# A gated attention and feed-forward decode step: half of w_down on 128 partitions, V's end and wo in fewer pieces

## The chip, the core and the metric

The kernel runs on one core of a Trainium2 chip. The metric is the device time in microseconds (us) of one execution: the median of the runs, beside which one execution is profiled. PE is the matrix engine, DVE the vector engine, ACT the scalar engine, POOL the general one, and SP the engine that issues nearly all transfers. The core's transfers run on 16 DMA engines.

## The reference

One token attends to a cache of 65,536 positions in 32 heads; beside it runs a gated feed-forward layer, and a scalar gate mixes the two.

```
x [1,1,512]; k_cache, v_cache [1,32,65536,128]; wq [512,4096]; wo [4096,512]
w_gate, w_up [512,1792]; w_down [1792,512]; all bf16

g = sigmoid((x * gate_w).sum())
q = (x @ wq) as 32 heads of 128
p = softmax(q . k_cache / sqrt(128));  o = p @ v_cache
a = o (as 4096 values) @ wo
b = (silu(x @ w_gate) * (x @ w_up)) @ w_down
out = g * a + (1 - g) * b
```

K and V are 512 MiB each and are read once.

## The kernel before, in words

**Tiles.** Each head's cache is cut into G = 4 parts of 16,384 rows, so there are N = 128 tiles of K and 128 of V. A tile is 4 MB: 128 partitions with 128 rows (32 KB) each. The tiles live in a ring of five slots (`take`, `give`); a load takes the slot that has been free longest, so SP waits there until PE or DVE has done with the slot's last content. Each transfer on SP also uses one of eight semaphores in turn, and waits until the transfer eight before it has landed.

**K.** `products` (L254, L258) multiplies a K tile by the head's query on DVE and folds it to 32 columns (64 for the first head); `scores` (L267) sums these with identity matmuls into PSUM, and `fold` (L281) sums the rest. After a head's four tiles come its maximum, the exponentials (`P_sb`) and the total.

**V.** `values` (L322) runs 32 matmuls for each V tile, four rows of each partition at a time. They accumulate in `O_ps`, [4, 512] for a head. `head_copy` (L335) and `head_turn` (L351, L358) turn that into one column of `oT`, scaled. For the last tile, the last TURNED = 8 rows go straight into the turned sum (L343). `project` (L365) multiplies a head's column by its 128 rows of wo, two matmuls of 256 columns that accumulate in `a_ps`.

**Order.** A list `steps` pairs K tile n with V tile v; K runs ahead. In each step SP issues K, then perhaps a wo group, then V; PE does a finished head's `head_turn`, then `values`, `scores` and `project`. wo comes in groups of WG = 4 heads (512 KB, rows of 1 KB) into a pool of two buffers, for the first 16 heads; for the last 16 heads (`LATE`), 2 MB come behind the last V in four pieces (L169) into a ring slot, and `project` for these 16 heads stands at the end of PE's program. The last three V tiles come in pieces too (`V_CUTS`): two halves, two halves, and rows 0, 32, 64, 96, 112, 120, 128 of the last.

**Feed-forward.** It runs in the first 100 us. SP issues, in this order: the first columns of wq, K 0 to 2, the rest of wq, w_gate, K 3, w_up, six pieces of w_down, K 4, two pieces of w_down, V 0, K 5, V 1 and so on. `feed_forward_in` (L178) makes the 14 + 14 columns of gate and up, `feed_forward_mid` their product `hT` [128, 14]. w_down lies on 64 partitions with 28 rows each. It comes in eight transfers (L402) of eight partitions: `firsts[i]`, and then every fourth. `feed_forward_out` regroups `hT` to 64 partitions by two matmuls (L227) and a copy (L231), and runs 28 matmuls (L233) over w_down; then the slot `wd_t` is given back, for which SP waits before K 6.

Of the kernel before, what the change touches and what calls it, by code (L numbers as in the profile page):

```python
# [8 lines left out]
ACT = mybir.ActivationFunctionType  # L9
ALU = mybir.AluOpType  # L10
AXIS = mybir.AxisListType
P = 128
# [3 lines left out]
NB = 128  # L16
# [7 lines left out]
SPREAD = 40  # L24

WG = 4
LATE = 16
LATE_CUTS = (0, 5, 10, 14, LATE)
TURNED = 8
V_CUTS = {3: (0, 64, NB), 2: (0, 64, NB), 1: (0, 32, 64, 96, 112, NB - TURNED, NB)}  # L30


@with_exitstack
def kernel(
# [14 lines left out]
    nc = tc.nc  # L49
    bf16 = mybir.dt.bfloat16  # L50
    f32 = mybir.dt.float32

    _, H, Sk, Dh = A_k_cache.shape
    D = A_x.shape[2]
    F = B_w_gate.shape[1]
    KT = D // P
    FT = F // P
    G = Sk // (NB * P)
    NBH = Sk // P
    N = H * G  # L60
    QG = 4
    assert Dh == P and Sk % (NB * P) == 0 and NBH <= 512 and H % QG == 0 and G >= 2
    scale = float(Dh) ** -0.5

    consts = ctx.enter_context(tc.tile_pool(name="consts", bufs=1))
# [7 lines left out]
    psum_m = ctx.enter_context(tc.tile_pool(name="psum_m", bufs=2, space=bass.MemoryType.PSUM))  # L73
# [7 lines left out]
    def take(name):  # L81
        slot = free.pop(0)
        held[name] = slot
        return ring.tile(
            [P, NB * Dh], bf16, name=name.split(".")[0], tag=f"slot{slot}"
        )
# [4 lines left out]
    xT = consts.tile([P, KT], bf16, name="xT")  # L91
# [24 lines left out]
    def load_v(n):  # L116
        load(V_tiles, A_v_cache, n, "V_t", V_CUTS.get(N - n, (0, NB)))

# [9 lines left out]
    ident_b = consts.tile([P, P], bf16, name="ident_b")  # L128
# [29 lines left out]
    wo_tiles = {}  # L158

    def load_wo(g):  # L160
        wo_tiles[g] = wo_pool.tile([P, WG, D], bf16, name="wo_sb", tag="wo_sb")
        rows = A_wo[g * WG * P : (g + 1) * WG * P, :]
        nc.sync.dma_start(out=wo_tiles[g], in_=rows.rearrange("(h p) n -> p h n", p=P))

    def load_late(cuts):
        late = take("wo_late.0")[:, : LATE * D].rearrange("p (h n) -> p h n", n=D)
        rows = A_wo[(H - LATE) * P :, :].rearrange("(h p) n -> p h n", p=P)
        for a, b in zip(cuts[:-1], cuts[1:]):
            nc.sync.dma_start(out=late[:, a:b, :], in_=rows[:, a:b, :])  # L169
        return late  # L170

    def feed_forward_in():
        gu_ps = psum_m.tile([P, 2 * FT], f32, name="gu_ps", tag="misc")
        for w in range(2):
            cols = wgu_sb[:, w].rearrange("p t (m c) -> p t c m", c=FT)
            for ft in range(FT):
                for t in range(KT):
                    nc.tensor.matmul(  # L178
                        gu_ps[:, w * FT + ft : w * FT + ft + 1],
                        lhsT=cols[:, t, ft, :],  # L180
                        rhs=xT[:, t : t + 1],
                        start=(t == 0),
                        stop=(t == KT - 1),
                    )
        gu_sb = consts.tile([P, 2 * FT], f32, name="gu_sb")
        nc.scalar.activation(out=gu_sb, in_=gu_ps, func=ACT.Copy)
        eg = consts.tile([P, FT], f32, name="eg")
        nc.scalar.activation(out=eg, in_=gu_sb[:, :FT], func=ACT.Exp, scale=-1.0)
        return gu_sb, eg

    def gate_sum():
# [22 lines left out]
    def feed_forward_mid(gu_sb, eg):  # L214
        nc.vector.tensor_scalar_add(eg, eg, 1.0)
        nc.vector.reciprocal(eg, eg)
        hprod = consts.tile([P, FT], f32, name="hprod")
        nc.vector.tensor_tensor(out=hprod, in0=gu_sb[:, :FT], in1=eg, op=ALU.mult)
        hT = consts.tile([P, FT], bf16, name="hT")
        nc.vector.tensor_tensor(out=hT, in0=hprod, in1=gu_sb[:, FT:], op=ALU.mult)  # L220
        return hT

    def feed_forward_out(hT, rest):
        b_ps = psum_m.tile([1, D], f32, name="b_ps", tag="misc")
        h_ps = psum_m.tile([HP, GT], f32, name="h_ps", tag="misc")
        for r in range(2):
            nc.tensor.matmul(  # L227
                h_ps[:, r * FT : (r + 1) * FT], lhsT=ident_b[:, r::2], rhs=hT, start=True, stop=True
            )
        h2 = consts.tile([HP, GT], bf16, name="h2")  # L230
        nc.scalar.activation(out=h2, in_=h_ps, func=ACT.Copy)  # L231
        for t in range(GT):
            nc.tensor.matmul(  # L233
                b_ps, lhsT=h2[:, t : t + 1], rhs=wd_sb[:, t, :], start=(t == 0), stop=(t == GT - 1)
            )
        nc.scalar.activation(out=b_sb, in_=b_ps, func=ACT.Copy, scale=rest)
        for i, a in enumerate(a_ps):
            nc.tensor.matmul(  # L238
                a, lhsT=ones_f[0:1, 0:1], rhs=b_sb[:, i * HD : (i + 1) * HD], start=True, stop=False
            )  # L240
# [36 lines left out]
    def fold(n):  # L277
        h, g = divmod(n, G)
        if g == 0:
            S_tiles[h] = small.tile([P, NBH], f32, name="S_sb")  # L280
        nc.vector.tensor_reduce(  # L281
# [12 lines left out]
    def exponentials(h, mT_ps):  # L294
# [3 lines left out]
        nc.scalar.activation(out=bias, in_=top, func=ACT.Copy, scale=-scale)  # L298
        P_tiles[h] = ppool.tile([P, NBH], bf16, name="P_sb")
        nc.scalar.activation(  # L300
# [15 lines left out]
    def values(n):  # L316
        h, g = divmod(n, G)
        if g == 0:
            O_tiles[h] = psum_o.tile([4, 4 * Dh], f32, name="O_ps")
        end = NB if n < N - 1 else NB - TURNED  # L320
        for j in range(0, end, 4):
# [38 lines left out]
        )  # L360

    def project(h):
        rows = wo_tiles[h // WG][:, h % WG, :] if h < H - LATE else wo_late[:, h - (H - LATE), :]
        for i, a in enumerate(a_ps):
            nc.tensor.matmul(  # L365
                a,
                lhsT=oT[:, h : h + 1],
                rhs=rows[:, i * HD : (i + 1) * HD],
                start=False,
                stop=(h == H - 1),  # L370
            )


    def score_tile(n):
        for _ in products(n):
            pass
        if n:
            fold(n - 1)
# [7 lines left out]
    wgu_sb = gu_t[:, : 2 * KT * F].rearrange("p (w t f) -> p w t f", w=2, t=KT)  # L386
# [4 lines left out]
    xs = gate_sum()  # L391
    scores(1)
    wd_t = take("wd_t.0")
    HP = P // 2
    GT = F // HP
    wd_sb = wd_t[:HP, : GT * D].rearrange("p (t n) -> p t n", t=GT)
    wd_rows = B_w_down.rearrange("(p t) n -> p t n", t=GT)
    firsts = (0, 1, 2, 3, 32, 33, 34, 35)

    def load_wd(i):  # L400
        part = slice(firsts[i], firsts[i] + 29, 4)
        nc.sync.dma_start(out=wd_sb[part], in_=wd_rows[part])  # L402

    for i in range(6):
        load_wd(i)
# [4 lines left out]
    load_k(4)  # L410
    load_wd(6)
    load_wd(7)
    score_tile(2)
    rest = gate_value(eg2)
    scores(2)
# [7 lines left out]
    v = 0  # L423
# [5 lines left out]
        steps.append((None, v))  # L429
        v += 1  # L430

    done = tot_ps = wo_late = None
    for n, v in steps:
        if n is not None and n > G:
            load_k(n)
        if v is not None:
            if v % (WG * G) == 2 and v // (WG * G) < (H - LATE) // WG:
                load_wo(v // (WG * G))
            if v:
                load_v(v)  # L440
            if v == N - 1:
                wo_late = load_late(LATE_CUTS)
        vector = iter(()) if n is None else products(n)
        top_of = None
        if n is None:
            top_of = H - 1 if F_tiles else None
        elif n % G == 0:
            top_of = n // G - 1
            vector = (i for a in (0, NB // 2) for i in products(n, a, a + NB // 2))
        if top_of is not None:  # L450
            next(vector, None)
            fold(top_of * G + G - 1)
            mT_ps = row_max(top_of)
            next(vector, None)
            exponentials(top_of, mT_ps)
        if n == G:
            hT = feed_forward_mid(*ff)
        for _ in vector:
            pass
        if n is not None and n % G:  # L460
            fold(n - 1)
        if tot_ps is not None:
            weight(*tot_ps)
            tot_ps = None
        if n == G:
            feed_forward_out(hT, rest)
            give("wd_t.0")
        if done is not None:
            head_turn(done, head_copy(done))
        if v is not None:  # L470
            values(v)
        if top_of is not None:
            tot_ps = top_of, total(top_of)
        if n is not None:
            scores(n)
        if done is not None and done < H - LATE:
            project(done)
        done = v // G if v is not None and v % G == G - 1 else None
    head_turn(H - 1, head_copy(H - 1))
    for h in range(H - LATE, H):  # L480
        project(h)

    out_sb = consts.tile([1, D], bf16, name="out_sb")
# [33 lines left out]
```

## Time and profile before

| | us |
|---|---|
| median of 3 runs (lowest, highest) | 2534.09 (2533.99, 2534.16) |
| the profiled execution's own time | 2534.41 |
| its span, first to last instruction | 2532.6 |
| moved | 1088.49 MB in 43,915 packets, mean 430 GB/s |
| PE busy, mean granted clock | 1533.7 (61%), 0.772 |
| DVE busy | 2083.7 (82%) |
| ACT, POOL busy | 77.7, 0.9 |
| instruction packets of 16 KB (queue q8) | 45 |

The span is 1.8 us shorter than the execution's own time. Times inside the trace count from the span's start. A busy share is a mean over the whole span; which transfer or engine ends last at one place has to be read there. The granted clock is PE's alone: 1.00 is full speed.

### The profile page before, as it was taken

The numbers are of one execution on the slowest core, as the hardware profiler recorded it, in microseconds if no ns is written. First come the engines' busy times: TensorE is split into PE (matmuls) and PEld (weight loads), VectorE is DVE, ScalarE is ACT, GpSimd is POOL, SyncE is SP. The second block draws the span as 40 slices with busy tenths as digits, with TensorE's granted clock in tenths as the row PEclk, the third lists the DMA queues.
The fourth block names the chain that finished last, engine by engine and source line by source line (L and its number), as shares of the span: only waits on it lengthen the run. The fifth ranks groups of instructions, "written<-read, shape, count | busy, mean of one in ns | idle before, by whom it ended". The sixth has DMA issues, their size and how long they took to land.

```text
span 2532.6 us, 13195 instructions
## 1 busy us (share of the span) xinstructions
PE 1533.7 (61%) x5786; PEld 581.6 (23%) x5786; DVE 2083.7 (82%) x744; ACT 77.7 (3%) x208; POOL 0.9 (0%) x7
## 2 busy tenths in 40 slices
PE   4656656665566555555665566556656665665569
PEld 1222222222222112222222122222222221222223
DVE  7788888888887999988888888888888888888860
ACT  1000000000000000000000000000000000000000
POOL 0000000000000000000000000000000000000000
PEclk9777777777777787787777777777777777777779
DMA  9999999999999999999999999999999999999998
GB/s 412 418 431 433 435 432 430 434 433 432 431 433 434 431 433 434 432 431 434 433 432 433 434 432 432 435 431 432 432 434 432 431 435 433 431 434 433 432 432 351
DMA packets 43915, 1088.49 MB, mean 430 GB/s; under 512 B 4753, under 2 KB 9362, under 8 KB 10258
## 3 DMA queue, kind: packets, MB, share of 16 engines
q1 hardware_dynamic: 43570, 1087.65, 99.7%
q8 instruction: 45, 0.74, 0.1%
q14 instruction: 12, 0.10, 0.0%
q10 hardware_dynamic: 288, 0.00, 0.0%
HBM read 1087.64 MB, written 0.00 MB: 429 GB/s over the span
## 4 chain that ended last, share of the span: by engine, by line
DMA 71%; PE 23%; DVE 4%; issue 1%; ACT 0%; SPq 0%; DVEq 0%
DMA V_t<-in_A_v_cache_dram 63%; PE O_ps L322 21%; DMA K_t<-in_A_k_cache_dram 8%; DVE K_t L254 3%; DVE K_t L258 1%; PE S_ps L267 1%; DMA wo_late<-in_A_wo_dram 0%; PE b_ps L233 0%; DVE S_sb L281 0%; DVE m L287 0%; PE oh_ps L351 0%; PE a_ps L238 0%; ACT P_sb L300 0%; PE a_ps L365 0%; PE mT_ps L291 0%
## 5 line engine op out<-in xcount | busy, mean ns | idle before, releaser
L322 PE MATMUL O_ps<-V_t,P_sb 128*4 128x512 bf16 x4094 | 1154.5, 452 | 663.5 <-DMA V_t<-in_A_v_cache_dram 663.5
L254 DVE TENSOR_TENSOR K_t<-K_t,q_bc 128x16384 bf16<-128x16384 bf16 (+1 forms) x159 | 1117.2, 7026 | 357.9 <-DMA K_t<-in_A_k_cache_dram 346.7
L258 DVE TENSOR_TENSOR K_t<-K_t 128x8192 bf16<-128x8192 bf16 (+1 forms) x314 | 859.7, 2738 | 8.6
L322 PEld LDWEIGHTS <-P_sb 128*4 128x4 bf16 x4094 | 393.0, 97 | 1405.1 <-issue 1064.1
L267 PE MATMUL S_ps<-K_t,ident_b 128*128 128x512 bf16 x1056 | 263.3, 393 | 100.6 <-DVE K_t L258 100.6
L267 PEld LDWEIGHTS <-ident_b 128*128 128x128 bf16 x1056 | 98.0, 101 | 248.0 <-issue 158.0
L291 PE MATMUL mT_ps<-diag,ones_f 128*128 128x128 f32 x64 | 24.5, 483 | 150.1 <-ACT diag L289 150.1
L351 PE MATMUL oh_ps<-ident_f,O_sb 4*128 4x1 f32 x256 | 55.5, 334 | 74.5 <-ACT O_sb L335 74.5
L281 DVE TENSOR_REDUCE S_sb<-S_ps 128x128 f32<-128x512 f32 x128 | 87.5, 683 | 4.9 <-PE S_ps L267 4.9
L289 ACT ACTIVATE diag<-ident_f,m 128x128 f32<-128x128 f32 x32 | 12.8, 401 | 2118.7 <-DVE m L287 2118.7
L351 PEld LDWEIGHTS oh_ps<-ident_f,O_sb 4*128 4x128 f32 x256 | 52.8, 301 | 84.1 <-ACT O_sb L335 82.9
L291 PEld LDWEIGHTS mT_ps<-diag,ones_f 128*128 128x128 f32 x64 | 15.2, 295 | 166.7 <-ACT diag L289 166.7
L484 DVE CAST out_sb<-a_ps 1x256 bf16<-1x256 f32 x1 | 0.4, 412 | 56.6 <-PE a_ps L365 56.6
L300 ACT ACTIVATE P_sb<-S_sb,bias 128x512 bf16<-128x512 f32 x32 | 23.1, 722 | 1.0
L287 DVE TENSOR_REDUCE m<-S_sb 128x1 f32<-128x512 f32 x32 | 22.0, 686 | 1.1
L335 ACT ACTIVATE O_sb<-O_ps 4x512 f32<-4x512 f32 x32 | 18.3, 572 | 129.2 <-PE O_ps L322 129.2
L313 DVE RECIPROCAL recip<-tot_ps 128x1 f32<-128x1 f32 x32 | 5.1, 158 | 13.0 <-PE tot_ps L308 13.0
L308 PEld LDWEIGHTS tot_ps<-rowsum,ones_f 128*128 128x128 f32 x64 | 9.5, 188 | 14.0 <-issue 14.0
L233 PE MATMUL b_ps<-wd_t,h 64*1 64x512 bf16 x28 | 12.1, 625 | 0.3 <-ACT h L231 0.3
L308 PE MATMUL tot_ps<-rowsum,ones_f 128*128 128x1 f32 x64 | 12.2, 260 | 0.0
L358 ACT ACTIVATE oT<-oh_ps,rg 128x1 bf16<-128x1 f32 x32 | 8.4, 263 | 65.0 <-PE oh_ps L351 65.0
L296 DVE TENSOR_REDUCE top<-mT_ps 128x1 f32<-128x128 f32 x32 | 9.1, 284 | 1.0 <-PE mT_ps L291 1.0
(47 smaller groups left out, 75.2 us busy)
## 6 DMA issues: line engine op xcount, KB each, us to landing
K_t<-in_A_k_cache_dram SPq DMA_DIRECT2D x128, 4096.0 KB, 35.3
V_t<-in_A_v_cache_dram SPq DMA_DIRECT2D x125, 4096.0 KB, 28.0
V_t<-in_A_v_cache_dram SPq DMA_DIRECT2D x4, 2048.0 KB, 31.1
wq_t<-in_A_wq_dram SPq DMA_DIRECT2D x1, 3584.0 KB
V_t<-in_A_v_cache_dram SPq DMA_DIRECT2D x3, 1024.0 KB
wo_sb<-in_A_wo_dram SPq DMA_DIRECT2D x4, 512.0 KB, 38.8
gu_t<-in_B_w_gate_dram SPq DMA_DIRECT2D x1, 1792.0 KB
gu_t<-in_B_w_up_dram SPq DMA_DIRECT2D x1, 1792.0 KB
```

Source lines behind the costliest of these rows:

```text
L254: yield nc.vector.tensor_tensor(out=K, in0=K, in1=q_rep, op=ALU.mult)
L258: yield nc.vector.tensor_tensor(out=K[:, :, 0:half], in0=K[:, :, 0:half], in1=K[:, :, half : 2 * half], op=ALU.add,)
L267: nc.tensor.matmul(S, lhsT=ident_b, rhs=K_tiles[n][:, :, c : c + QUAD], start=(c == 0), stop=(c == width - QUAD),)
L281: nc.vector.tensor_reduce(out=S_tiles[h][:, g * NB : (g + 1) * NB], in_=F_tiles.pop(n), axis=AXIS.X, op=ALU.add)
L287: nc.vector.tensor_reduce(out=m, in_=S_tiles[h], axis=AXIS.X, op=ALU.max)
L289: nc.scalar.activation(out=diag, in_=ident_f, func=ACT.Copy, scale=m)
L291: nc.tensor.matmul(mT_ps, lhsT=ones_f, rhs=diag, start=True, stop=True)
L300: nc.scalar.activation(out=P_tiles[h], in_=S_tiles[h], func=ACT.Exp, bias=bias, scale=scale, accum_out=rowsum[:, h : h + 1],)
L308: nc.tensor.matmul(tot_ps, lhsT=ones_f, rhs=rowsum[:, h : h + 1], start=True, stop=True)
L322: nc.tensor.matmul(O_tiles[h], lhsT=P_tiles[h][:, g * NB + j : g * NB + j + 4], rhs=V_tiles[n][:, j : j + 4, :], start=(g == 0 and j == 0) ...
L335: nc.scalar.activation(out=O_sb, in_=O_tiles.pop(h), func=ACT.Copy)
L351: nc.tensor.matmul(oh_ps, lhsT=O_sb[:, c * Dh : (c + 1) * Dh], rhs=ident_f[0:4, c : c + 1], start=(c == 0 and not turned), stop=(c == 3),)
```

## The change

w_down's first 896 rows lie on 64 partitions, 14 rows each, and come by the same eight transfers, half as long. The other 896 rows lie on all 128 partitions, 7 rows each, and come by one transfer issued behind the last small one. `feed_forward_in` forms its columns in the order that this wants: 7 columns with steps of 7, 14 with steps of 14. In the latter only the first 64 rows are used, so there are 21 columns for each of gate and up instead of 14. `feed_forward_out` has 21 matmuls, without the regrouping. All 32 heads' wo rows come in groups of four: groups 0 to 6 in the stream, group 7 behind the last V, in one transfer. Only the last four heads are projected at the end. The last V tile comes in five pieces instead of six.

```diff
-LATE = 16
-LATE_CUTS = (0, 5, 10, 14, LATE)
 TURNED = 8
-V_CUTS = {3: (0, 64, NB), 2: (0, 64, NB), 1: (0, 32, 64, 96, 112, NB - TURNED, NB)}
+V_CUTS = {3: (0, 64, NB), 2: (0, 64, NB), 1: (0, 32, 64, 96, NB - TURNED, NB)}
...
-    FT = F // P
+    HP = P // 2
+    HALF = F // P
+    ALL = (F - HALF * HP) // P
+    FC = HALF + ALL
...
-            cols = wgu_sb[:, w].rearrange("p t (m c) -> p t c m", c=FT)
-            for ft in range(FT):
+            for c in range(FC):
+                out = gu_ps[:, w * FC + c : w * FC + c + 1]
                 for t in range(KT):
+                    cols = wgu_sb[:, w, t, :]
+                    rows = cols[:, HALF * HP + c :: ALL] if c < ALL else cols[:, c - ALL :: HALF]
                     nc.tensor.matmul(
-                        gu_ps[:, w * FT + ft : w * FT + ft + 1],
-                        lhsT=cols[:, t, ft, :],
...
+                        out, lhsT=rows, rhs=xT[:, t : t + 1], start=(t == 0), stop=(t == KT - 1)
...
-        for r in range(2):
-            nc.tensor.matmul(
-                h_ps[:, r * FT : (r + 1) * FT], lhsT=ident_b[:, r::2], rhs=hT, start=True, stop=True
-            )
-        h2 = consts.tile([HP, GT], bf16, name="h2")
-        nc.scalar.activation(out=h2, in_=h_ps, func=ACT.Copy)
-        for t in range(GT):
-            nc.tensor.matmul(
-                b_ps, lhsT=h2[:, t : t + 1], rhs=wd_sb[:, t, :], start=(t == 0), stop=(t == GT - 1)
-            )
+        for c in range(FC):
+            nc.tensor.matmul(
+                b_ps,
+                lhsT=hT[: P if c < ALL else HP, c : c + 1],
+                rhs=wd_all[:, c, :] if c < ALL else wd_half[:, c - ALL, :],
+                start=(c == 0),
+                stop=(c == FC - 1),
             )
...
-        rows = wo_tiles[h // WG][:, h % WG, :] if h < H - LATE else wo_late[:, h - (H - LATE), :]
+        rows = wo_tiles[h // WG][:, h % WG, :]
...
-    wd_sb = wd_t[:HP, : GT * D].rearrange("p (t n) -> p t n", t=GT)
-    wd_rows = B_w_down.rearrange("(p t) n -> p t n", t=GT)
+    wd_half = wd_t[:HP, : HALF * D].rearrange("p (t n) -> p t n", t=HALF)
+    wd_all = wd_t[:, HALF * D : FC * D].rearrange("p (t n) -> p t n", t=ALL)
+    rows_half = B_w_down[: HALF * HP, :].rearrange("(p t) n -> p t n", t=HALF)
+    rows_all = B_w_down[HALF * HP :, :].rearrange("(p t) n -> p t n", t=ALL)
...
     load_wd(6)
     load_wd(7)
+    nc.sync.dma_start(out=wd_all, in_=rows_all)
...
-            if v % (WG * G) == 2 and v // (WG * G) < (H - LATE) // WG:
+            if v % (WG * G) == 2 and v // (WG * G) < H // WG - 1:
                 load_wo(v // (WG * G))
             if v:
                 load_v(v)
             if v == N - 1:
-                wo_late = load_late(LATE_CUTS)
+                load_wo(H // WG - 1)
...
-        if done is not None and done < H - LATE:
+        if done is not None and done < H - WG:
             project(done)
...
-    for h in range(H - LATE, H):
+    for h in range(H - WG, H):
         project(h)
```

More of the change, by code (lines that the diff above doesn't have):

```diff
@@ L163, in load_wo @@
         nc.sync.dma_start(out=wo_tiles[g], in_=rows.rearrange("(h p) n -> p h n", p=P))
[L165 to L170, printed above, removed]
     def feed_forward_in():
-        gu_ps = psum_m.tile([P, 2 * FT], f32, name="gu_ps", tag="misc")
+        gu_ps = psum_m.tile([P, 2 * FC], f32, name="gu_ps", tag="misc")
         for w in range(2):
-            cols = wgu_sb[:, w].rearrange("p t (m c) -> p t c m", c=FT)
-            for ft in range(FT):
+            for c in range(FC):
+                out = gu_ps[:, w * FC + c : w * FC + c + 1]
                 for t in range(KT):
+                    cols = wgu_sb[:, w, t, :]
+                    rows = cols[:, HALF * HP + c :: ALL] if c < ALL else cols[:, c - ALL :: HALF]
                     nc.tensor.matmul(
-                        gu_ps[:, w * FT + ft : w * FT + ft + 1],
-                        lhsT=cols[:, t, ft, :],
-                        rhs=xT[:, t : t + 1],
-                        start=(t == 0),
-                        stop=(t == KT - 1),
+                        out, lhsT=rows, rhs=xT[:, t : t + 1], start=(t == 0), stop=(t == KT - 1)
                     )
-        gu_sb = consts.tile([P, 2 * FT], f32, name="gu_sb")
+        gu_sb = consts.tile([P, 2 * FC], f32, name="gu_sb")
         nc.scalar.activation(out=gu_sb, in_=gu_ps, func=ACT.Copy)
-        eg = consts.tile([P, FT], f32, name="eg")
-        nc.scalar.activation(out=eg, in_=gu_sb[:, :FT], func=ACT.Exp, scale=-1.0)
+        eg = consts.tile([P, FC], f32, name="eg")
+        nc.scalar.activation(out=eg, in_=gu_sb[:, :FC], func=ACT.Exp, scale=-1.0)
         return gu_sb, eg
@@ L216, in feed_forward_mid @@
         nc.vector.reciprocal(eg, eg)
[L217 to L220, printed above, removed]
+        hprod = consts.tile([P, FC], f32, name="hprod")
+        nc.vector.tensor_tensor(out=hprod, in0=gu_sb[:, :FC], in1=eg, op=ALU.mult)
+        hT = consts.tile([P, FC], bf16, name="hT")
+        nc.vector.tensor_tensor(out=hT, in0=hprod, in1=gu_sb[:, FC:], op=ALU.mult)
         return hT
@@ L224, in feed_forward_out @@
         b_ps = psum_m.tile([1, D], f32, name="b_ps", tag="misc")
-        h_ps = psum_m.tile([HP, GT], f32, name="h_ps", tag="misc")
-        for r in range(2):
+        for c in range(FC):
             nc.tensor.matmul(
-                h_ps[:, r * FT : (r + 1) * FT], lhsT=ident_b[:, r::2], rhs=hT, start=True, stop=True
-            )
-        h2 = consts.tile([HP, GT], bf16, name="h2")
-        nc.scalar.activation(out=h2, in_=h_ps, func=ACT.Copy)
-        for t in range(GT):
-            nc.tensor.matmul(
-                b_ps, lhsT=h2[:, t : t + 1], rhs=wd_sb[:, t, :], start=(t == 0), stop=(t == GT - 1)
+                b_ps,
[3 more added lines that the diff above has]
+                stop=(c == FC - 1),
             )
@@ L393 @@
     wd_t = take("wd_t.0")
-    HP = P // 2
-    GT = F // HP
-    wd_sb = wd_t[:HP, : GT * D].rearrange("p (t n) -> p t n", t=GT)
-    wd_rows = B_w_down.rearrange("(p t) n -> p t n", t=GT)
+    wd_half = wd_t[:HP, : HALF * D].rearrange("p (t n) -> p t n", t=HALF)
+    wd_all = wd_t[:, HALF * D : FC * D].rearrange("p (t n) -> p t n", t=ALL)
+    rows_half = B_w_down[: HALF * HP, :].rearrange("(p t) n -> p t n", t=HALF)
+    rows_all = B_w_down[HALF * HP :, :].rearrange("(p t) n -> p t n", t=ALL)
     firsts = (0, 1, 2, 3, 32, 33, 34, 35)
@@ L401, in load_wd @@
         part = slice(firsts[i], firsts[i] + 29, 4)
-        nc.sync.dma_start(out=wd_sb[part], in_=wd_rows[part])
+        nc.sync.dma_start(out=wd_half[part], in_=rows_half[part])
     for i in range(6):
@@ L430 @@
         v += 1
-    done = tot_ps = wo_late = None
+    done = tot_ps = None
     for n, v in steps:
```

## Prediction

> **What bounds the kernel now.** I read the page first: DMA at nine tenths in every slice, DVE at 82%, PE at 61%. Then the chain of waits and, for the last 45 us, the timeline.
>
> ```profile
> DMA  9999999999999999999999999999999999999998
> DMA 71%; PE 23%; DVE 4%; issue 1%; ACT 0%; SPq 0%; DVEq 0%
> ```
>
> In order of time (start, length, what) the chain ends so:
>
> ```profile
> 2516.42 12.18 DMA wo_late<-in_A_wo_dram
> 2528.60 0.04 issue
> 2528.65 1.48 PE a_ps L365 x12
> ```
>
> The transfers set the pace, and the end: the last matmuls (L365) start when the third piece of wo_late lands (2528.60), then come the copy and the store. The timeline of the end gives PE's part:
>
> ```profile
> 2521.35 3.18 PE L322 MATMUL O_ps<-V_t,P_sb 128*4 128x512 bf16 x14 [0.28 <-DMA V_t<-in_A_v_cache_dram]
> 2524.63 0.59 ACT L335 ACTIVATE O_sb<-O_ps 4x512 f32<-4x512 f32 x1 [28.74 <-PE O_ps L322]
> 2526.25 3.87 PE L365 MATMUL a_ps<-wo_late,oT 128*1 128x256 bf16 x32
> 2530.15 0.37 ACT L485 ACTIVATE out_sb<-a_ps 1x256 bf16<-1x256 f32 x1 [3.54 <-PE a_ps L365]
> ```
>
> Yet the DMA engines are not busy there. The stretches show it (columns: stretch and length; busy PE, PEld, DVE, ACT, POOL with counts; granted clock; DMA share; GB/s):
>
> ```profile
> 2518.00:2520.00 2.00, 2.00 (x11) 0.77 (x9) 0.00 (x0) 0.00 (x0) 0.00 (x0) 1.00 0.73 268
> 2520.00:2522.00 2.00, 1.72 (x9) 0.59 (x8) 0.00 (x0) 0.00 (x0) 0.00 (x0) 1.00 0.38 137
> 2524.00:2528.00 4.00, 3.54 (x36) 2.60 (x35) 0.00 (x0) 0.85 (x2) 0.00 (x0) 1.00 0.38 123
> ```
>
> Some of the 16 engines have finished and others are late. The trace also holds each landing's semaphore steps, one per engine; read off there (us, first and last engine):
>
> ```
> transfer                            first    last    spread
> K tile 3, before any w_down         56.45    56.94     0.5
> K tile 4, behind six w_down pieces  70.52    78.36     7.8   (eight by 70.84, eight from 76.75)
> V tile of 130 us                   123.97   130.80     6.8
> last V tile, rows 64 to 96        2507.36  2521.30    13.9
> last V tile, rows 120 to 128      2509.92  2523.84    13.9
> wo_late, last piece               2525.57  2529.27     3.7
> ```
>
> So eight engines carry w_down alone (each piece has eight data steps), and one of these eight, call it E, is last ever after. Followed landing by landing, E is never dry: 9.67 us per 4 MB tile, without a gap. Its lag also grows by 1.5 us at about 490, 959, 1427, 1893 and 2340 us, right after 16 KB reads of the instruction queue (q8). A tile counts as landed when E has it, so what E carries is what counts.
>
> **The change, part by part, on E.**
> w_down. Today E moves eight packets of 28,672 B; the pieces land 1.06 us apart: 8.5 us. After, it moves eight of 14,336 B (the w_gate load is eight such packets, 47.27 - 42.96 = 4.31 us) and eight of 7,168 B from the 128-partition transfer (wq_rest is 32 such, 8.94 us, so 2.24). Sum 6.55: 1.95 us less. The other eight engines get 2.24 more, and they lead by 5 to 6.
>
> wo. Three more groups (4 to 6) go ahead of the last V: the three mid-stream wo loads of the trace cost E 1.32, 1.33 and 1.34, so +4.0. Behind V, 1.36 (512 KB) remain of 1.71 + 1.69 + 1.36 + 0.67 = 5.43. So V's end lands 4.0 - 1.95 = 2.05 us later than now, and the queue ends 2.0 earlier, at 2527.25.
>
> V. Rows 96 to 120 in one piece take the 1.26 + 0.63 of the two pieces now. They land at 2523.19 + 2.05 = 2525.24, rows 64 to 96 at 2523.35, the last eight at 2525.9. The number of transfers stays 22 in these parts (8 + 4 + 6 + 4 before, 9 + 8 + 5 after), so SP issues as many.
>
> PE at the end. Eight L322 (0.216 each: 32 in 7.07 with the last one's tail) from 2523.40 to 2525.12, then six from 2525.29, of which the last starts at 2526.37 (now 2524.15). From there to the first L365 it takes 2526.25 - 2524.15 = 2.10 today, through O_sb, L351 and oT; nothing of it changes: 2528.47. Then only 8 of the 32 L365 are left, 0.109 apart: the last starts at 2529.23, today at 2529.84. That is 0.6 us gained, and wo's landing at 2527.25 no longer ends last: PE behind the last V does. The 24 L365 that move into the stream (2.6 us) lie in PE's idle time, 39% of the span.
>
> Feed-forward, all around 60 to 100 us, from the groups (busy, mean ns | idle before) and from SP's waits (us in total, times, longest):
>
> ```profile
> L233 PE MATMUL b_ps<-wd_t,h 64*1 64x512 bf16 x28 | 12.1, 625 | 0.3 <-ACT h L231 0.3
> L178 PEld LDWEIGHTS <-gu_t 128*128 128x128 bf16 x112 | 6.9, 162 | 0.2
> ```
>
> ```profile
> SPq L110 <- PE b_ps L233: 19.5, 1, 19.5
> ```
>
> L178 grows from 112 to 168 matmuls: 56 x 0.062 = 3.5 us on PE, up to twice that at half clock. It delays scores(3) by at most 7 us, and behind it SP's K 5 and V 1 loads (issued at 66.84 and 76.28). E's queue then still holds K 4, w_down and V 0, to 88: covered by over 10 us. If that cover were gone, each us late would be a us lost. L233 falls from 28 to 21 (0.43 each, -3.0 us), and L227 and L231 go (-0.55). K 6, which waits for them on SP until 100.10, is issued some 3.5 us sooner, or 6 with w_down's earlier landing; E does not need it before 107. Gain nothing: E was not dry. The leading engines were (2.6 us), and that costs nothing.
>
> New waits: load_wo(7) waits for an earlier V landing on its semaphore and for a wo buffer whose projection ended some 30 V tiles before; behind it on SP stands only the store. The mid-stream wo loads go ahead of a V load on SP: 0.43 us each of issuing, with E some 28 us behind the issue.
>
> Unknown costs. One 24-row piece instead of two: between 0 and 0.05 less. The strided weights of L178 (step 7 and 14, all 14 before): bounded by zero and by PE's cover. Reads of instructions: PE's program has 94 instructions more, so 45 or 46 instead of 45; E takes every eighth, so one more or one less than now is possible: +1.5 or -1.5, I take none, as six now fall on E at numbers 0, 8 ... 40.
>
> Sum: the span of 2532.6 becomes 2532.0; with the 1.8 us outside the span, 2533.8 for this execution (2534.4 before); as the median of the runs lies 0.3 lower, 2533.5. A measurement of this kernel can tell about 0.2% from no change, 5.1 us, so this is "no change".
>
> **The rivals.**
> Fixed price per transfer. The first wq load, alone, lands 3.94 us after its issue, where 512 KB of wo take 1.36 in the queue: 2.6 us a transfer if nothing hid it. One V piece less before the last V would then give 2.6 more: 2530.9. Against it: pieces of 640, 640, 512 and 256 KB took 1.71, 1.69, 1.36 and 0.67 behind one another, proportional, no fixed part. [...]
>
> The instruction reads move off E. They took 1.5 us five times since 130 us. If their rotation falls on other engines in the new program, the next late one of the eight ends 3.6 us before E: V lands that much sooner, 2529.9, or a little below 2529. For it: the program gets longer; against: the rotation counts from the start, which is unchanged.
>
> The last engine is not of the eight. Then w_down adds 2.24 to it instead of taking 1.95, V lands 4.2 later than I say, and the end comes 3.6 us later than now: 2537.7. It decides from the point where the other eight's lead is under 4.2 us. Against: the late group of eight appears exactly with the w_down pieces, and I can follow its last member to the end.
>
> PE falls to half clock in the tail. The windows give 0.51 for 78 to 100 us, where L233 takes 0.43 a matmul, and 1.00 after 2468. Half rate from the second half of the last tile but one (2516): 46 matmuls at 0.427 instead of 0.216 add 9 us, the small ones 1.8: 2544. It costs over 0.2% if it begins before about 2523. Against: the waits for V there (1.06 and 0.28 us) stay as they are. [...]
>
> **How the numbers follow.** Forecast 0.74 (its own range 2531.9 to 2536.7: one read less; one read more and one slow clock window of 3.4 us, which costs 1.7), reads off E 0.09, fixed price 0.04, other engine 0.06, clock 0.07. The range reaches down to 2529.9 and up to 2536.7 and leaves out the other engine, the clock and half of the reads' case, 0.17. Faster by over 0.2% is that half (0.04), slower the clock (0.07), the rest within.
>
> **What would show it.** Right: landings behind the six w_down pieces spread by about 4 us, not 7.8; the last V tile's pieces land 2.05 later than now, wo's last at about 2527.2; six L322 wait for rows 96 to 120; eight L365 at the end, and the chain ends over V and PE, not over wo. Wrong: a growing number of 1.5 us steps on E, a clock under 1.00 after 2468, or an idle E (a tile's landing more than 9.7 us after the one before without such a step).

## The result, and the profile after

| | before | after |
|---|---|---|
| median of the runs beside each other (lowest, highest), us | 2534.12 (2532.63, 2534.20) | 2541.93 (2541.70, 2543.29) |
| ratio, 95% interval | | 1.0034 (1.0023 to 1.0044) |
| profiled execution, its span, us | 2534.41, 2532.6 | 2543.28, 2541.5 |

The changed kernel is 0.34% slower, 7.8 us by the medians. The forecast was 2533.5 with a range up to 2536.7: it was wrong. The runs of most kernels here fall into two groups some 1.5 us apart (2532.6 and 2534.1 before, 2541.8 and 2543.3 after) and a median can stand for either, so between like groups the change costs 9.2 us.

The chain of waits in order of time (start, length, what) now ends so:

```profile
2498.44 34.43 DMA V_t<-in_A_v_cache_dram
2532.91 3.33 PE O_ps L311 x14
2536.33 0.59 ACT O_sb L324
2536.97 1.05 PE oh_ps L340 x8
2538.01 0.98 PE a_ps L354 x8
2539.02 0.37 ACT out_sb L475
```

That is the chain that was foretold: it ends over the last V tile and PE, no longer over wo. L311 is the former L322, L354 the former L365. The timeline has the waits that were foretold as well:

```profile
2532.91 3.32 PE L311 MATMUL O_ps<-V_t,P_sb 128*4 128x512 bf16 x14 [0.29 <-DMA V_t<-in_A_v_cache_dram]
2537.95 1.03 PE L354 MATMUL a_ps<-wo_sb,oT 128*1 128x256 bf16 x8
```

Eight matmuls wait for rows 64 to 96, six more for rows 96 to 120, and eight of L354 remain. Every interval in this tail is as worked out; only the whole of it stands 9.5 us too late. So the time was not lost here. The stretches (stretch and length; busy PE, PEld, DVE, ACT, POOL with counts; granted clock; DMA share; GB/s) show the tail at full clock:

```profile
2528.00:2530.00 2.00, 2.00 (x11) 0.77 (x10) 0.00 (x0) 0.00 (x0) 0.00 (x0) 1.00 0.66 262
2530.00:2532.00 2.00, 2.00 (x11) 0.77 (x9) 0.00 (x0) 0.00 (x0) 0.00 (x0) 1.00 0.45 168
2532.00:2534.00 2.00, 1.71 (x9) 0.60 (x8) 0.00 (x0) 0.00 (x0) 0.00 (x0) 1.00 0.14 56
```

and the same view over the long middle, first of before, then of after, shows where it was lost:

```profile
200.00:2400.00 2200.00, 1315.57 (x4844) 493.95 (x4843) 1879.03 (x662) 62.15 (x172) 0.00 (x0) 0.76 1.00 433
```

```profile
200.00:2400.00 2200.00, 1308.05 (x4820) 491.17 (x4820) 1868.57 (x659) 61.94 (x171) 0.00 (x0) 0.76 1.00 431
```

The DMA engines are busy all the time in both (share 1.00), but move 431 GB/s instead of 433, in a part of the kernel where the change adds only three wo groups and their matmuls. PE and DVE do less in it because less arrives; their instructions are not slower. The products on DVE, first of before, then of after (busy, mean ns | idle before):

```profile
L254 DVE TENSOR_TENSOR K_t<-K_t,q_bc 128x16384 bf16<-128x16384 bf16 (+1 forms) x159 | 1117.2, 7026 | 357.9 <-DMA K_t<-in_A_k_cache_dram 346.7
L243 DVE TENSOR_TENSOR K_t<-K_t,q_bc 128x16384 bf16<-128x16384 bf16 (+1 forms) x159 | 1117.3, 7027 | 369.0 <-DMA K_t<-in_A_k_cache_dram 364.3
```

The page has the same packets and bytes as before, only at a lower mean:

```profile
DMA packets 43915, 1088.49 MB, mean 428 GB/s; under 512 B 4753, under 2 KB 9362, under 8 KB 10258
```

The semaphore steps of the landings, counted on the first engine of each transfer, say how it comes about. The step from one 4 MB tile to the next is 9.681 us before (median) and 9.712 after. It is there from the start: the median of the first 20 tiles behind K 7 is 9.681 and 9.713, long before a piece of V's end is issued. (K 1 lands 9.68 us after K 0 before and 9.71 after, ahead of all of w_down, but these first steps differ from execution to execution, from 9.66 to 9.88 in runs with the step of before, so that one pair alone shows nothing.) The landings stand so:

```
transfer (us)                             forecast   after (last engine)
K tile 4, spread behind six w_down pieces   about 4       4.8 (7.8 before)
last V tile, rows 64 to 96               2523.35     2532.87
last V tile, rows 96 to 120              2525.24     2534.73
last group of wo                         2527.25     2536.78
```

So every one of the 253 whole tiles costs 0.031 us more: 253 x 0.031 = 7.8 us, most of the 9.5. What can change the price of a transfer whose own line is the same? The addresses at which it lands. They are those of the built program, not of a trace. The constants of the feed-forward have grown (`gu_sb` from 112 to 168 bytes a partition, `eg` and `hprod` from 56 to 84, `hT` from 28 to 42; `h2` with 56 is gone), each is rounded up to 32, and so all that lies behind them moves by 96 bytes. The ring of the five slots began at byte 30,976 of each partition, which is 121 x 256; now it begins at 31,072. The slots are 32,768 apart, so all five are off by the same 96. The two wo buffers have moved by 96 too.

### The profile page after: what moved, and what is told of

Its sections match the earlier page's. It is cut to its first block, busy times and chain, and to the rows that moved or that the text cites. A ratio compares the mean times of both kernels' runs of the same rounds, so it can differ in the third digit from the quotient of the medians.

```text
span 2541.5 us, 13284 instructions
## 1 busy us (share of the span) xinstructions
PE 1534.3 (60%) x5833; PEld 583.5 (23%) x5833; DVE 2083.8 (82%) x744; ACT 77.6 (3%) x207; POOL 0.9 (0%) x7
## 4 chain that ended last, share of the span: by engine, by line
DMA 72%; PE 22%; DVE 5%; issue 0%; ACT 0%; SPq 0%; DVEq 0%; ACTq 0%
DMA V_t<-in_A_v_cache_dram 65%; PE O_ps L311 21%; DMA K_t<-in_A_k_cache_dram 7%; DVE K_t L243 3%; DVE K_t L247 2%; PE S_ps L256 1%; DVE S_sb L270 0%; PE oh_ps L340 0%; DVE m L276 0%; ACT P_sb L289 0%; ACT O_sb L324 0%; PE mT_ps L280 0%; PE a_ps L354 0%; DVE top L285 0%; ACT diag L278 0%
## 5 line engine op out<-in xcount | busy, mean ns | idle before, releaser
L311 PE MATMUL O_ps<-V_t,P_sb 128*4 128x512 bf16 x4094 | 1155.4, 452 | 682.5 <-DMA V_t<-in_A_v_cache_dram 682.5
L311 PEld LDWEIGHTS <-P_sb 128*4 128x4 bf16 x4094 | 393.7, 97 | 1422.0 <-issue 1079.9
L354 PE MATMUL a_ps<-wo_sb,oT 128*1 128x256 bf16 x64 | 11.9, 275 | 0.0
```

The source lines that it names most:

```text
L311: nc.tensor.matmul(O_tiles[h], lhsT=P_tiles[h][:, g * NB + j : g * NB + j + 4], rhs=V_tiles[n][:, j : j + 4, :], start=(g == 0 and j == 0) ...
```

## The experiments

The theory: a row that lands at an address off a multiple of 256 bytes costs its DMA engine some 4 ns more (0.031 us a tile over the eight rows of an engine), and that is all that went wrong; the recorded sum holds beside it. Its rivals: the loss belongs to w_down's two layouts (the strided weights, two loads in one slot); or to V's end and wo; or only to the wo buffers' address, not to the ring's.

**e1: the changed kernel, the ring put back on a multiple of 256 (31,232).**

```diff
 # behind b_sb, in the pool of constants
+    pad = consts.tile([P, 40], f32, name="pad")
+    nc.vector.memset(pad[0:1, 0:1], 0.0)
```

> The changed kernel with 160 bytes of padding in the constants, so that the ring's slots begin at byte 31,232 of a partition (a multiple of 256) instead of 31,072 (96 more than one). Theory A, the address: every row that a transfer writes costs some 5 ns more when it does not begin on such a boundary. Then a 4 MB tile takes 9.68 us per landing again instead of 9.71, and the time is what the recorded sum says without that step, 2533.5. Theory B, the work: the split of w_down or the wo groups in the stream slow the transfers. Theory C, the longer program: it lies, or puts the inputs, elsewhere in HBM. By B and C the time stays at 2541.9 and a tile at 9.71.

Measured: 2533.12 us (2531.57 to 2533.39), 0.9995 of before (0.9986 to 1.0005). A tile's step is 9.681 again. The stretch of the middle and the timeline of the end:

```profile
200.00:2400.00 2200.00, 1313.56 (x4855) 493.33 (x4855) 1875.03 (x662) 62.22 (x172) 0.00 (x0) 0.76 1.00 433
```

```profile
2523.01 3.31 PE L313 MATMUL O_ps<-V_t,P_sb 128*4 128x512 bf16 x14 [0.30 <-DMA V_t<-in_A_v_cache_dram]
2528.03 1.03 PE L356 MATMUL a_ps<-wo_sb,oT 128*1 128x256 bf16 x8
```

433 GB/s are back, and the end stands where the prediction had put it: rows 96 to 120 land at 2524.82 (2525.24 said), wo at 2526.81 (2527.25), the last eight matmuls start at 2528.03 (2528.47). 160 bytes of padding a partition take 2541.93 to 2533.12: 8.8 us by the medians, which here belong to different groups, and 10.2 between like groups. It is a rate: the first engine of the changed kernel lands V 30, 60, 90 and 120 later than in e1 by 2.0, 4.3, 6.5 and 8.5 us.

**e2: the kernel before, with nothing but its ring and wo moved by 96 bytes.**

```diff
+    pad = consts.tile([P, 24], f32, name="pad")
+    nc.vector.memset(pad[0:1, 0:1], 0.0)
```

> The kernel before with 96 bytes of padding, so that its ring begins at 31,072 as in the changed kernel; the work is the same. A: 9.71 us per tile from the first tile on, 250 tiles at 0.03 us more, so 2534.1 + 7.5 to 8 = 2541.6 to 2542.1. B: 2534.1. C: 2534.1, the program is as long as before but for one small instruction.

Measured: 2543.11 us (2542.25 to 2544.03), ratio 1.0038 (1.0023 to 1.0053); a tile's step 9.712. The stretch of the middle and the end of the chain:

```profile
200.00:2400.00 2200.00, 1299.77 (x4808) 490.06 (x4808) 1873.97 (x660) 62.20 (x172) 0.00 (x0) 0.76 1.00 431
```

```profile
2523.97 12.47 DMA wo_late<-in_A_wo_dram
2536.49 1.48 PE a_ps L367 x12
```

Without w_down's new layout and without the new tail, the address alone costs 9.1 us (9.5 and 9.9 between like groups), over 1 us more than I expected, since I had counted only the tiles. A group of wo pays as well (1.46 to 1.49 us where it was 1.33 to 1.39), w_gate and w_up a little (4.27 and 4.30, before 4.25 and 4.26); wq's load shows nothing of it (8.77, before 9.01). Whether these make up all that is left over was not worked out. The chain still ends over wo, as in the kernel before (2528.65), 7.8 us later; this trace is of the lower group, and that of before of the upper. Rivals one and two fall as causes of the loss, and theory C of the expectations with them: e1 keeps the longer program and does not lose, e2 keeps the short one and does.

**e5, e6, e7: the same with 32, 64 and 128 bytes** (`pad` of 8, 16 and 32 columns): is it any address off 256, or does a smaller multiple do?

> The kernel before with its ring moved by 32 bytes (31,008: 32 past a multiple of 64 and of 256). If the boundary that counts is 64 bytes or more: 9.71 us a tile, about 2543. If any multiple of 32 will do and something else is at work at 96: 9.68 and 2534.

> Ring moved by 64 bytes (31,040: a multiple of 64, 64 past one of 256). A with a boundary of 64: 9.68 us a tile and 2534. A with a boundary of 128 or 256: 9.71 and 2543.

> Ring moved by 128 bytes (31,104: 128 past a multiple of 256). Boundary of 64 or 128: 9.68 us a tile and 2534. Boundary of 256: 9.71 and 2543.

| ring moved by | us (before beside it) | ratio (95%) | a tile's step, us |
|---|---|---|---|
| 0 | 2534.06 | | 9.681 |
| 32 (e5) | 2546.61 | 1.0050 (1.0028 to 1.0073) | 9.720 |
| 64 (e6) | 2544.36 | 1.0040 (1.0020 to 1.0060) | 9.712 |
| 96 (e2) | 2543.11 (before 2534.05) | 1.0038 (1.0023 to 1.0053) | 9.712 |
| 128 (e7) | 2543.87 | 1.0037 (1.0022 to 1.0053) | 9.713 |

(e2's median lies between its two groups of runs; the step is the better measure.) Being on a multiple of 32, 64 or 128 is not enough; 0 and e1's 256 are the only cheap ones of those tried. The price is one of rows, not of bytes. An engine moves eight rows of each V or K transfer (32,384 packets of 32 KB for 253 tiles on 16 engines), and the steps of the transfers cut to shorter rows grow as much as those of the long ones:

```
row      on 256        off 256          per row
32 KB    9.681 us      9.712, 9.720     3.9 to 4.9 ns
16 KB    4.854         4.890 to 4.906   4.5 to 6.5
 8 KB    2.45          2.48 to 2.49     3 to 5
 1 KB    1.35 to 1.37  1.47 to 1.485    3 to 4 (wo: 32 rows an engine)
```

By that, an engine's 253 whole tiles make 2,024 rows x 3.9 ns, the same 7.8 us, and the eight groups of wo 256 x 3.5 = 0.9, together 8.7 before the few rows of V's last pieces and of the weights. The first engine of the last wo group lands 2523.23 - 2514.22 = 9.0 us later after the change than in e1.

**e8: only the wo buffers moved by 96 bytes, the ring left on 256** (the padding lies in the pool `small`, behind the ring):

```diff
+    pad = small.tile([P, 24], f32, name="pad", bufs=1)
+    nc.vector.memset(pad[0:1, 0:1], 0.0)
```

> 96 bytes of padding behind the ring instead of before it: the ring stays on a multiple of 256, while the small tiles, the probabilities and the wo pool lie 96 bytes later, as in the changed kernel. If the ring's address carries the cost: 9.68 us a tile and 2534.2 at most (four wo loads of 32 rows an engine at 3 ns: 0.4 us). If another tile's address does (the sums, P_sb, the wo pool): 2543.

Measured: 2534.11 us, ratio 1.0000 (0.9989 to 1.0012).

```profile
200.00:2400.00 2200.00, 1314.48 (x4840) 493.60 (x4840) 1879.03 (x662) 62.18 (x172) 0.00 (x0) 0.76 1.00 433
```

The middle is that of before. A 512 KB group of wo takes 1.41 to 1.49 us instead of 1.33 to 1.39, so these rows do pay; but only four groups go to these buffers in the kernel before, some 0.5 us in all. The loss is carried by the ring: rival three falls.

**e3: w_down's part alone, the ring on 256; e4: V's end and wo alone, the ring where it was.** Do the two halves of the recorded sum hold each for itself?

```diff
 # e3, against the changed kernel
+LATE = 16
+LATE_CUTS = (0, 5, 10, 14, LATE)
-V_CUTS = {3: (0, 64, NB), 2: (0, 64, NB), 1: (0, 32, 64, 96, NB - TURNED, NB)}
+V_CUTS = {3: (0, 64, NB), 2: (0, 64, NB), 1: (0, 32, 64, 96, 112, NB - TURNED, NB)}
+    pad = consts.tile([P, 40], f32, name="pad")
+    nc.vector.memset(pad[0:1, 0:1], 0.0)
...
-                load_wo(H // WG - 1)
+                wo_late = load_late(LATE_CUTS)
```

> The w_down part of the change alone (with the padding that puts the ring on a multiple of 256), the end of V and wo as before. A and the sum on the last engine: V and wo land 1.95 us sooner, the end as well: 2532.1 to 2532.3. B with w_down as the cause: about 2541. C: about 2541, the program is as long as the changed one.

Measured: 2531.61 us, ratio 0.9991 (0.9982 to 1.0001): 2.4 us less than before, where 1.95 were worked out for w_down. Nine of the ten runs lie between 2530.12 and 2531.75. One took 3404.07 us and is left out of the ratio; why it did is open.

```diff
 # e4, against the changed kernel: w_down on 64 partitions again
-    wd_half = wd_t[:HP, : HALF * D].rearrange("p (t n) -> p t n", t=HALF)
-    wd_all = wd_t[:, HALF * D : FC * D].rearrange("p (t n) -> p t n", t=ALL)
+    wd_sb = wd_t[:HP, : GT * D].rearrange("p (t n) -> p t n", t=GT)
...
-    nc.sync.dma_start(out=wd_all, in_=rows_all)
```

> V's end and wo in fewer pieces alone, w_down as before; the ring lies on a multiple of 256 as before. A and the sum: V lands 4.0 us later than before, rows 96 to 120 at about 2527.2, and the end comes 1.3 us later than before: 2535.4, at 9.68 us a tile. B with wo as the cause: over 2540. C: about 2534 to 2536, the program is shorter than the changed one.

Measured: 2535.58 us, ratio 1.0006 (0.9996 to 1.0015), 1.5 more than before. Its timeline:

```profile
2525.14 3.29 PE L313 MATMUL O_ps<-V_t,P_sb 128*4 128x512 bf16 x14 [0.53 <-DMA V_t<-in_A_v_cache_dram]
2530.15 1.03 PE L356 MATMUL a_ps<-wo_sb,oT 128*1 128x256 bf16 x8
```

V comes 3.8 us later than before (rows 64 to 96 at 2525.14 against 2521.35; 4.0 were worked out for three groups of wo), and the shorter work behind it gives back most of that. The three groups themselves took 1.33, 1.30 and 1.33 us on the last engine, 3.96 in all. That V's delay is so near to it is in part luck: a step of 1.55 us in the lag, of the size that the instruction reads had, falls on rows 32 to 64 of the last tile here and on other places in before. So w_down gives 2.4, the tail takes 1.5, and their sum is -0.9; e1 has both and stands 0.93 below before. The intervals of both ratios reach 1. What speaks for the two numbers is that they come out alike in both groups of runs (-2.5 and -2.6, +1.5 and +1.5). The landings in single traces can't carry them: e3's trace, of the lower group, has V 4.1 us sooner than that of before.

**e9: all of w_down on 128 partitions, by one transfer.** The w_down pieces in eight transfers of eight partitions put eight engines behind for the rest of the kernel: in the trace of before the first and the last engine are 9.9 us apart behind all of w_down, 13.9 at the last V tile. If that lag is the price, the even layout should take it away:

```diff
-    wd_sb = wd_t[:HP, : GT * D].rearrange("p (t n) -> p t n", t=GT)
-    wd_rows = B_w_down.rearrange("(p t) n -> p t n", t=GT)
-    firsts = (0, 1, 2, 3, 32, 33, 34, 35)
...
+    wd_sb = wd_t[:, : FT * D].rearrange("p (t n) -> p t n", t=FT)
+    nc.sync.dma_start(out=wd_sb, in_=B_w_down.rearrange("(p t) n -> p t n", t=FT))
...
-                b_ps, lhsT=h2[:, t : t + 1], rhs=wd_sb[:, t, :], start=(t == 0), stop=(t == GT - 1)
+                b_ps, lhsT=hT[:, t : t + 1], rhs=wd_sb[:, t, :], start=(t == 0), stop=(t == FT - 1)
...
+    pad = consts.tile([P, 16], f32, name="pad")   # the ring stays on 30,976
+    nc.vector.memset(pad[0:1, 0:1], 0.0)
```

> All of w_down on 128 partitions by one transfer (14 rows each), no regrouping, 14 matmuls; the end of V and wo as in the kernel before; 64 bytes of padding keep the ring on a multiple of 256. The sum on the last engine: eight packets of 14,336 B (4.3 us) in place of eight of 28,672 (8.5), so everything behind lands 4.2 us sooner: 2529.8 to 2530.0. Rival: the last engine is bound elsewhere (by the other eight, which now carry 4.3 us more each, or by a dry queue around 100 us): 2532 to 2534.

Measured: 2529.81 us (2529.67 to 2530.09), ratio 0.9984 (0.9975 to 0.9993). Near its end the chain reads:

```profile
2482.41 34.37 DMA V_t<-in_A_v_cache_dram
2516.82 3.20 PE O_ps L317 x14
2521.79 2.27 PE a_ps L360 x20
2524.11 1.48 PE a_ps L360 x12
```

The spread between the engines behind all of w_down is 1.9 us (9.9 before, 5.9 in the changed kernel), and the last piece of wo lands at 2524.70, 4.6 us sooner than before. It is faster than both kernels, by 4.3 us than before (3.0 against the lower group of before; its own runs make one group) and by 12.1 than the changed one, which did not run beside it. And it is the simplest of the three: no regrouping, 14 matmuls, one transfer.

## Why the prediction was wrong, point by point

- **The failed step** is one that the prediction made without a word: it held the price of a tile at 9.67 us (9.68 by the medians), the rate of the trace of before, and listed as unknown only the 24-row piece, the strided weights and the instruction reads. The diff enlarges four constants and drops one. They stand ahead of the ring, so it moved 96 bytes off its multiple of 256. That had no place in the sum, and it cost 8.8 us (e1; 10.2 between like groups), more than twice the largest term that was there. The step from 9.681 to 9.712 us a tile makes 7.8 of it; the wo groups' rows add some 0.9.
- **What would show it** named the sign rightly ("a tile's landing more than 9.7 us after the one before without such a step") and its cause wrongly: it was put down to an idle E. E was busy; each of its rows took longer (9.712 us a tile instead of 9.681, at a DMA share of 1.00 from 200 to 2400 us).
- **None of the rivals came about.** No transfer's fixed price was saved (in e1 rows 96 to 120 land 0.42 us sooner than worked out, not 2.6); the last engine's lag still grew five times by 1.5 to 1.7 us in the profiled execution, so the reads did not move off it there; it stayed one of the eight (the spread behind six pieces of w_down shrank from 7.8 to 4.8, about 4 said); the clock is 1.00 in the tail, from 2478.4 to 2539.6 us; and what the forecast missed was a rate over the whole span, where the four rivals were events at a few places.
- **The slow clock window of 3.4 us, +1.7** in the range's upper end: stretches of that length at 0.50 are in the trace of before (863.7 to 867.1 us, 1017.3 to 1020.7), but the traces of before and of the changed kernel show none in the tail. Before grants 1.00 from 2468 to 2532 us, the changed kernel from 2478.4 to 2539.6, and its last matmul ends at 2539.0.
- **w_down on E, -1.95.** In the changed kernel's trace the small pieces land 0.54 us apart and the 128-partition transfer 2.17 after the last of them: 8 x 0.54 + 2.17 = 6.5 against 6.55. By the runs -2.4 (e3); where the other half us comes from is open.
- **wo ahead of the last V, +4.0.** The three groups took 3.96 in e4's trace. In the changed kernel itself each group took 1.47 rather than 1.32 to 1.34, since its rows lie off 256.
- **V's end and PE's end, -0.6.** Right to 0.4 us at every point of e1, and in the changed kernel right in every interval behind the landing.
- **Feed-forward: gain nothing, lose nothing.** SP's waits in the changed kernel (us in total, times, longest):

```profile
SPq L111 <- PE b_ps L218: 12.7, 1, 12.7
SPq L111 <- PE gu_ps L174: 5.1, 1, 5.1
```

  The wait for `b_ps` was 19.5 and K 6 is issued at 91.50 us instead of 100.10, more than the 3.5 to 6 us that were worked out, and it gained nothing, as said. The wait for the 168 matmuls of L174 grew from 1.3 to 5.1: K 5 was issued at 69.94 instead of 66.84, within the 7 us that were bounded and the 10 of cover.
- **The sum**, 2533.5: e1 measured 2533.12. It was right for the changed kernel with its ring on a multiple of 256.

## What to carry to other kernels

An edit that changes the size of any buffer moves every buffer behind it, so before the terms of a change are added up, the addresses of the large transfers' targets are compared between the two built programs. Where the transfers set the pace, put large buffers on multiples of 256 bytes (96 bytes off took 9.1 us of 2534 in e2), by padding as here or by placing them ahead of the small ones (not tried), and look at the step between equal transfers first when a kernel gets slower: a loss that begins with the first tiles has not come from the end. Spread a load over all DMA engines: w_down on eight of 16 left these behind to the end, since the queue of the last of them never ran dry (9.9 us behind w_down, 13.9 at the last V tile); on all 16 the kernel took 4.3 us less (e9).

## What the runs showed of the hardware that was not expected

- A row that lands 32, 64, 96 or 128 bytes off a multiple of 256 in on-chip memory cost its engine about 4 ns more (3.9 to 4.9 with 32 KB, 3 to 4 with 1 KB); here 0.3 to 0.5% of the whole time. The packets' own mean time shows it faintly: 1,214 ns for 32 KB on the boundary, 1,218 off it. Of the offsets tried, 32 costs most (4.9 ns). Why, stays open, and offsets over 128 were not tried.
- The stretch of the middle shows 32 bytes as little as 96; the dearest case has to be read from the landings or from the time:

```profile
200.00:2400.00 2200.00, 1313.71 (x4797) 491.12 (x4797) 1871.04 (x659) 61.93 (x171) 0.00 (x0) 0.76 1.00 431
```

  This is e5, 3.5 us slower than e2 by the medians (2.7 than e2's upper group), with the same 431 GB/s.
- Of the 9.9 us by which rows 96 to 120 land later in the changed kernel than in e1, the first engine shows 8.9. The other 1.0 is lag that the last engine gathered, 0.3 of it by the first V tile; where the rest came from was not tried. One lead is in the traces: a 16 KB packet of the instruction queue took 0.93 us in the mean before and in e1, and 1.07 in the changed kernel and in e2.
- The two groups of runs are 1.5 us apart, the size of one instruction read on the last engine, as seen five times in the trace of before. The traces hint at which reads make them. Behind the first piece of w_down its eight engines lie 1.5 to 1.8 us apart in before, in the changed kernel, in e1 and in e5 to e8, none of them known to be of the lower group; in e2 and e3, both of the lower group, 0.2. There the read at 60 us seems to have fallen on an engine outside the eight. e4's trace, of the upper group, has 0.4 and the late step of 1.55 instead. In e9, where all 16 engines carry w_down, the runs don't split. Whether it is so in every run is not shown.
